# A fused linear-attention and feed-forward kernel: another order of the pair visits from stage 10 on

## The chip, the cores and the metric

The kernel runs on one core of one Trainium2 chip. The core has five engines with instruction streams of their own: TensorE (PE), which multiplies matrices into PSUM; VectorE (DVE) and ScalarE (ACT), which work element by element and can read PSUM; GpSimd (POOL), which here builds tiles in SBUF and issues loads; and SyncE (SP), which issues transposes and stores. They meet only at semaphores. The metric is the device time of one execution in microseconds; all times below are microseconds unless another unit stands beside them.

## The reference

For each batch and head a state of 48 x 48 is carried along 768 tokens (linear attention with a decay `w` and a bonus `u` for the present token). The result, 3072 x 384, goes through two dense products with a leaky ReLU between them.

```python
B, H, S, D = 4, 8, 768, 48
for t in range(S):
    cur = einsum('bhd,bhe->bhde', u * k[t], v[t])
    y[t] = einsum('bhd,bhde->bhe', r[t], state + cur)
    state = w[:, :, None] * state + einsum('bhd,bhe->bhde', k[t], v[t])
x = y.transpose(0, 2, 1, 3).reshape(3072, 384)
h = x @ w_in            # 384 -> 2048
out = maximum(0.01 * h, h) @ w_out   # 2048 -> 384
```

## The kernel before

**Stages.** The 768 tokens are cut into 6 chunks of 128, for 4 batches: 24 stages, numbered chunk by chunk, so stage n uses the state that stage n - 4 left. From about stage 8 on the stages are worked in pairs.

**Tokens of the order.** All work is recorded from one long string, `ORDER` (lines 27 to 52): each token calls a function that adds operations, and each engine executes its own operations in the order in which the string added them. The tokens that matter here, n being a stage (for J a pair):

- `k`, `r`, `v` n: loads, issued by POOL (L241).
- `Pnq`, `Pnk`: DVE scales r and k with decay tables (L390). `XnT`: SP transposes both by DMA into `tp` (L395).
- `qn`: three DVE operations, ku (L419), rku (L421) and a reduction to `s_tok` (L423), the weights of the present token. `Qn`: two POOL operations write them as diagonal tiles into `at` (L430).
- `An`: scores on PE, 8 matmuls into two PSUM banks (L482). `Mna`, `Mnb`: DVE copies the masked scores over the diagonal tiles in `at` (L495).
- `Kn`: key-value products on PE, 4 matmuls into one bank (L523). `Sn`: two DVE operations, one that adds the bank to the old state (L589) and one that applies the decay (L591). The result is the state of stage n + 4.
- `Yn`: the attention's output on PE, 28 matmuls in 32-column strips (L621) from v, `at`, `tp` and the state. `yn`: ACT copies it to `xT` (L635).
- `Jp.i`: an eighth of the first dense product of pair p on PE, 6 matmuls into one bank (L660); `jp.i`: ACT applies the leaky ReLU into `gT` (L671). It reads `xT` of both stages of the pair.
- `Hn`: the second dense product of stage n on PE, 16 matmuls into one bank (L684); `hn`: ACT copies it (L696) and SP stores it (L698). It needs all of `gT` of its stage.

**Waits.** `Sched` notes who wrote and who read each buffer and gives an operation waits on those of other engines that it needs. An engine executes in order, so an operation that waits holds up all behind it.

**PSUM banks.** The eight banks are a list. `take()` takes the first entry and `give()` appends one at its end. Both are called while the string is read: a bank given back by `Sn` is marked free from that place of the string on, and whoever takes it next waits for the operation that read it last. `Sn` calls `give` for the bank of `Kn`, `Mna` and `Mnb` for those of `An`, and `yn`, `jp.i` and `hn` for theirs.

Of the kernel before, what the change touches and what calls it, by code (L numbers as in the profile page):

```python
# [26 lines left out]
ORDER = """  # L27
w8 qk0 k0 v0z one r0 trow ones v0y tcol wlz r1 id8 F9 wi1 u8 zr table Cw Wl id E w bc lnw c0q@ T0q c0k@ tri u exps k1
T0k u16 wu8 Cu t0q t0k qtab P1q F6 k3 v3 U A0 ktab T1q v0 t1q X0 C D0 P1k T1k t1k F4 M0b P3k M0a T3k K3 utab X1 A1 D1
Q0 Y0 t3k P0k r3 P3q M1a T3q r2 P2q y0 k2 K0 M1b v1 Q1 W G0.1 Y1 t3q X3 wi3 A3 y1 g0.1 S3 T2q D3 G1.1 g1.1 k5 t2q r5 r4  # L30
P2k T2k wi2 S0 v2 M3b t2k Q3 G0.3 g0.3 G1.3 k4 M3a Y3 P5k A2 y3 P4q T4q v4 wi0 T5k v5 wo3 t4q g1.3 G3.1 q5 t5k Q5 G3.3
g3.3 P5q r6 wo2 X2 g3.1 M2b D2 wo1 G3.2 Q2 G0.2 g0.2 T5q t5q K2 P4k T4k M2a t4k S2 G1.2 g3.2 q4 Q4 K1 S1 Y2 A5 A4 G1.0
y2 G2.1 M5a G0.0 G2.3 M4a M5b Y5 g0.0 y5 M4b Y4 y4 G2.2 g2.2 K4 J2.4 j2.4 k6 wo0 J2.1 J2.2 g1.0 g1.2 S4 k7 P6q q6 j2.1
P6k P7k G2.0 r7 q7 X6T J2.6 j2.6 J2.3 j2.3 k8 G3.0 J2.7 j2.7 k9 r9 j2.2 J2.5 P7q g3.0 g2.3 X7T J2.0 H1 h1 r8 q8 g2.0 Q6
P9k j2.0 P8k H0 j2.5 H3 Q7 A6 P9q X9T P8q X8T v6 A7 M6a v7 M7a g2.1 H2 h2 v9 v11 v10 M6b Y6 M7b y6 Q8 q9 Y7 y7 K5 r11
K6 S6 r10 k10 S5 Q9 v8 K7 S7 h0 h3 k11 J3.0 j3.0 J3.1 j3.1 J3.2 j3.2 J3.3 j3.3 J3.4 j3.4 J3.5 j3.5 J3.6 j3.6 J3.7 j3.7
A8 A9 M8a M8b M9a M9b P10q P10k X10T P11q P11k X11T k12 r12 v12 k13 r13 v13 q10 Q10 q11 Q11 H4 h4 Y8 Y9 y8 y9 K8 K9 S8
S9 H5 h5 J4.0 j4.0 J4.1 j4.1 J4.2 j4.2 J4.3 j4.3 J4.4 j4.4 J4.5 j4.5 J4.6 j4.6 J4.7 j4.7 A10 A11 M10a M10b M11a M11b
P12q P12k X12T P13q P13k X13T k14 r14 v14 k15 r15 v15 q12 Q12 q13 Q13 H6 h6 Y10 Y11 y10 y11 K10 K11 S10 S11 H7 h7 J5.0
j5.0 J5.1 j5.1 J5.2 j5.2 J5.3 j5.3 J5.4 j5.4 J5.5 j5.5 J5.6 j5.6 J5.7 j5.7 A12 A13 M12a M12b M13a M13b P14q P14k X14T  # L40
P15q P15k X15T k16 r16 v16 k17 r17 v17 q14 Q14 q15 Q15 H8 h8 Y12 Y13 y12 y13 K12 K13 S12 S13 H9 h9 J6.0 j6.0 J6.1 j6.1
J6.2 j6.2 P16q P16k X16T P17q P17k X17T A14 A15 J6.3 j6.3 M14a M14b M15a M15b k18 r18 v18 k19 r19 v19 J6.4 j6.4 J6.5
j6.5 J6.6 j6.6 J6.7 j6.7 q16 Q16 q17 Q17 H10 h10 Y14 Y15 y14 y15 K14 K15 S14 S15 H11 h11 J7.0 j7.0 J7.1 j7.1 J7.2 j7.2
P18q P18k X18T P19q P19k X19T A16 A17 J7.3 j7.3 M16a M16b M17a M17b k20 r20 v20 k21 r21 v21 J7.4 j7.4 J7.5 j7.5 J7.6
j7.6 J7.7 j7.7 q18 Q18 q19 Q19 H12 h12 Y16 Y17 y16 y17 K16 K17 S16 S17 H13 h13 J8.0 j8.0 J8.1 j8.1 J8.2 j8.2 P20q P20k
X20T P21q P21k X21T A18 A19 J8.3 j8.3 M18a M18b M19a M19b k22 r22 v22 k23 r23 v23 J8.4 j8.4 J8.5 j8.5 J8.6 j8.6 J8.7
j8.7 q20 Q20 q21 Q21 H14 h14 Y18 Y19 y18 y19 K18 K19 S18 S19 H15 h15 J9.0 j9.0 J9.1 j9.1 J9.2 j9.2 P22q P22k X22T P23q
P23k X23T A20 A21 J9.3 j9.3 M20a M20b M21a M21b J9.4 j9.4 J9.5 j9.5 J9.6 j9.6 J9.7 j9.7 q22 Q22 q23 Q23 H16 h16 Y20 Y21
y20 y21 H17 h17 J10.0 j10.0 J10.1 j10.1 J10.2 j10.2 A22 A23 J10.3 j10.3 M22a M22b M23a M23b J10.4 j10.4 J10.5 j10.5
J10.6 j10.6 J10.7 j10.7 H18 h18 Y22 Y23 y22 y23 H19 h19 J11.0 j11.0 J11.1 j11.1 J11.2 j11.2 J11.3 j11.3 J11.4 j11.4  # L50
J11.5 j11.5 J11.6 j11.6 J11.7 j11.7 H20 h20 H21 h21 H22 h22
"""


# [750 lines left out]
```

## Time and profile before

| what | value |
|---|---|
| runs | 168.78, 168.86, 168.94 us; median 168.86 us |
| span of the profiled execution, first to last instruction | 166.8 us |
| instructions in it | 4840 |
| PE busy | 160.2 us |
| DVE, ACT, POOL busy | 107.6, 89.0, 111.0 us |
| granted TensorE clock, mean | 1.000 |

The profiled execution is one execution of the same program; its span leaves out what lies ahead of the first and behind the last instruction. In the rows of the timeline the first number is the start, counted from the span's beginning, the second the time from there to the end of the last of the merged instructions (`x16` means 16 of them), and a bracket at the end tells how long the engine was idle before the row and who released it. PEld is TensorE's loading of weights, which runs beside its matmuls. Ends of matmuls are modelled, so the prediction measures blocks of PE from start to start.

### The profile page before, as it was taken

What the parts mean: (1) busy time and instruction counts of PE and PEld (TensorE: products, weight loads), DVE (VectorE), ACT (ScalarE), POOL (GpSimd) and SP (SyncE); (2) the same over time, 40 slices, a digit from 0 to 9 for tenths busy, and PEclk for the clock granted to TensorE, in tenths of its full rate; (3) what the DMA queues carried; (4) which work ended last, traced back from release to release, by engine and by line L of the source; (5) the groups of instructions that cost most, each with busy time, mean ns of one, the idle gap of its engine ahead of it and who ended that gap; (6) DMA issues with size and microseconds to landing.
All of it is one profiled execution on the core that took longest, in us unless ns stands there. A gap on an engine that the chain in (4) does not pass through costs nothing.

```text
span 166.8 us, 4840 instructions
## 1 busy us (share of the span) xinstructions
PE 160.2 (96%) x2076; PEld 120.6 (72%) x2076; DVE 107.6 (64%) x224; ACT 89.0 (53%) x168; POOL 111.0 (67%) x125
## 2 busy tenths in 40 slices
PE   2899989999999999999999999999999999999994
PEld 2578879986567678678678678678678678678663
DVE  7799998478687695695699998865765705000000
ACT  3846973875048339339337437437437447449121
POOL 8999898978999949859759979896630630000000
PEclk9999999999999999999999999999999999999999
DMA  7999999999999994996994999999917011011012
GB/s 109 156 140 157 169 193 192 171 149 173 93 168 220 113 157 130 105 108 155 105 146 118 152 127 127 156 140 140 154 51 165 12 47 51 0 47 51 35 59 96
DMA packets 101267, 20.18 MB, mean 121 GB/s; under 512 B 94459, under 2 KB 101246, under 8 KB 101246
## 3 DMA queue, kind: packets, MB, share of 16 engines
q0 software_dynamic: 76512, 10.03, 95.0%
q1 hardware_dynamic: 23694, 9.65, 29.1%
q8 instruction: 16, 0.26, 0.7%
q10 hardware_dynamic: 1040, 0.20, 0.6%
q14 instruction: 5, 0.04, 0.1%
HBM read 20.45 MB, written 4.72 MB: 151 GB/s over the span
## 4 chain that ended last, share of the span: by engine, by line
PE 86%; POOL 7%; DMA 3%; DVE 2%; issue 0%; ACT 0%; POOLq 0%
PE ps L684 38%; PE ps L660 36%; PE ps L621 6%; DMA r_sb<-in_r_dram 3%; PE ps L482 3%; PE ps L523 2%; POOL r_sb L241 2%; POOL k_sb L241 2%; POOL v_sb L241 2%; POOL w_in_sb L251 1%; DVE prod L405 1%; DVE s_tok L423 0%; PE ps L453 0%; POOL trow L273 0%; DVE rku L421 0%
## 5 line engine op out<-in xcount | busy, mean ns | idle before, releaser
L660 PE MATMUL ps<-xT,w_in_sb 128*128 128x256 bf16 (+1 forms) x672 | 67.2, 257 | 0.0
L684 PE MATMUL ps<-w_out_sb,gT 128*128 128x384 bf16 (+2 forms) x400 | 65.6, 320 | 0.0
L671 ACT ACTIVATE gT<-ps 128x512 bf16<-128x512 f32 x96 | 56.3, 598 | 13.8 <-PE ps L660 9.7
L660 PEld LDWEIGHTS ps<-xT,w_in_sb 128*128 128x128 bf16 x672 | 57.1, 98 | 7.5 <-DVE sum_t L589 0.5
L430 POOL TENSOR_TENSOR at<-ident,s_tok 128x512 bf16<-128x512 bf16 x40 | 42.7, 1096 | 23.4 <-DVE s_tok L423 23.4
L684 PEld LDWEIGHTS ps<-w_out_sb,gT 128*128 128x128 bf16 x400 | 37.7, 98 | 22.4
L696 ACT ACTIVATE out_sb<-ps 128x384 f32<-128x384 f32 (+2 forms) x25 | 11.8, 477 | 54.5 <-PE ps L684 54.5
L495 DVE CAST_PREDICATED at<-mask,ps 128x512 bf16<-128x512 uint16 x40 | 24.9, 684 | 21.3 <-PE ps L482 21.2
L241 POOL DMA_DIRECT2D v_sb<-in_v_dram x24 | 22.1, 927 | 0.0
L241 POOL DMA_DIRECT2D k_sb<-in_k_dram x23 | 21.2, 925 | 0.0
L241 POOL DMA_DIRECT2D r_sb<-in_r_dram x23 | 21.1, 924 | 0.1
L421 DVE TENSOR_TENSOR rku<-r_sb,ku 128x384 bf16<-128x384 bf16 x20 | 13.8, 688 | 1.1 <-DMA r_sb<-in_r_dram 0.5
L589 DVE TENSOR_TENSOR sum_t<-ps,st 128x384 bf16<-128x384 f32 x16 | 8.8, 550 | 5.6 <-PE ps L523 5.6
L635 ACT ACTIVATE xT<-ps 128x384 bf16<-128x384 f32 x24 | 10.8, 490 | 2.6 <-PE ps L621 2.6
L423 DVE TENSOR_REDUCE s_tok<-rku 128x8 f32<-128x384 bf16 x20 | 11.1, 553 | 0.7
L591 DVE TENSOR_TENSOR st<-sum_t,wl 128x384 bf16<-128x384 bf16 x16 | 10.6, 664 | 0.6
L621 PE MATMUL ps<-at,v_sb 128*32 128x128 bf16 x384 | 10.8, 223 | 0.0
L390 DVE TENSOR_TENSOR qk<-k_sb,ktab 128x384 bf16<-128x384 bf16 x23 | 10.1, 444 | 1.1 <-DMA k_sb<-in_k_dram 1.1
L621 PEld LDWEIGHTS ps<-tp,st 128*32 128x32 bf16 x240 | 7.3, 96 | 3.0 <-issue 1.6
L621 PEld LDWEIGHTS ps<-at,v_sb 128*32 128x32 bf16 x384 | 8.8, 98 | 0.5 <-issue 0.2
L621 PE MATMUL ps<-tp,st 128*32 128x128 bf16 x240 | 9.1, 221 | 0.0
L390 DVE TENSOR_TENSOR qk<-r_sb,qtab 128x384 bf16<-128x384 bf16 x23 | 8.8, 386 | 0.2 <-DMA r_sb<-in_r_dram 0.2
(63 smaller groups left out, 92.9 us busy)
## 6 DMA issues: line engine op xcount, KB each, us to landing
out_dram<-out_sb SPq DMA_DIRECT2D x23, 192.0 KB, 2.2
v_sb<-in_v_dram POOLq DMA_DIRECT2D x24, 96.0 KB, 4.8
r_sb<-in_r_dram POOLq DMA_DIRECT2D x23, 96.0 KB, 4.7
k_sb<-in_k_dram POOLq DMA_DIRECT2D x23, 96.0 KB, 4.9
w_in_sb<-in_moe_w_in_dram POOLq DMA_DIRECT2D x4, 384.0 KB, 6.1
w_out_sb<-in_moe_w_out_dram POOLq DMA_DIRECT2D x4, 384.0 KB, 7.1
tp<-qk SPq DMA_TRANSPOSE x18, 5.3
k_f<-in_k_dram ACTq DMA_DIRECT2D x1, 192.0 KB, 2.8
```

Source lines behind the costliest of these rows:

```text
L241: add("pool", lambda: G.dma_start(dst, src), R=pace, W=[(which, n)], dma=f"{which}{n}")
L390: add("dve", lambda: V.tensor_tensor(qk[iq][:, H * half:H * half + H, 0:D], hd(src), hd(tab[:, :]), ALU.mult), R=[(name, n), "qk"[half] + ...
L421: add("dve", lambda: V.tensor_tensor(rku[i2][:, :], r_of(n), ku[i2][:, :], ALU.mult), R=[("r", n), ("ku", i2)], W=[("rku", i2)])
L423: add("dve", lambda: V.tensor_reduce(s_tok[i2][:, :], hd(rku[i2][:, :]), AX.X, ALU.add), R=[("rku", i2)], W=[("s", i2)])
L430: add("pool", lambda hh=hh, s_of=s_of: G.tensor_tensor(at[ia][:, hh, :, :], ident[:, :].unsqueeze(1).to_broadcast([128, NP, 128]), s_of.un ...
L495: add("dve", lambda: V.copy_predicated(at[n % NAT][:, hh, :, :], mask[:, :].bitcast(mybir.dt.uint16).unsqueeze(1).to_broadcast([128, NP, 1 ...
L621: last = PE.matmul(ps_y[32 * q:32 * q + 32, 128 * s:128 * s + 128], a, m, start=not whole and step == 0, stop=step == len(columns[q]) - 1)
L635: add("act", lambda: A.activation(xT[ix][:, :, 128 * slot:128 * slot + 128], ps_y[:, 0:HD].rearrange("p (s t) -> p s t", t=128), AF.Copy), ...
L660: last = PE.matmul(ps_g[:, step * f:step * f + step], w_in_sb[:, s, 128 * fb:128 * fb + 128], xT[ix][:, s, t], start=s == 0, stop=s == NSL ...
L671: add("act", lambda: A.activation(gT[ig][:, fb0:fb0 + count, t], ps_g[:, :].rearrange("p (f t) -> p f t", t=128 * width), AF.Prelu, alpha= ...
L684: last = PE.matmul(ps_o[:, 0:c1 - c0], gT[ig][:, s, 128 * slot:128 * slot + 128], w_out_sb[:, s, c0:c1], start=s == 0, stop=s == NFB - 1)
L696: add("act", lambda: A.activation(out_sb[io][:, c0:c1], ps_o[:, 0:c1 - c0], AF.Copy), R=[key], W=held)
```

## The change

Only the string is changed, from the end of J4 (the first dense product of stages 8 and 9) on. Before, the scores of a pair stand behind or inside the first products, in a visit of their own, and the other visit is H, both Y, both K, H:

```diff
 J4.0 j4.0 J4.1 j4.1 J4.2 j4.2 J4.3 j4.3 J4.4 j4.4 J4.5 j4.5 J4.6 j4.6 J4.7 j4.7
-A10 A11 M10a M10b M11a M11b P12q P12k X12T P13q P13k X13T k14 r14 v14 k15 r15 v15 q12 Q12 q13 Q13
-H6 h6 Y10 Y11 y10 y11 K10 K11 S10 S11 H7 h7
-J5.0 j5.0 J5.1 j5.1 J5.2 j5.2 J5.3 j5.3 J5.4 j5.4 J5.5 j5.5 J5.6 j5.6 J5.7 j5.7
-A12 A13 M12a M12b M13a M13b P14q P14k X14T P15q P15k X15T k16 r16 v16 k17 r17 v17 q14 Q14 q15 Q15
-H8 h8 Y12 Y13 y12 y13 K12 K13 S12 S13 H9 h9
-J6.0 j6.0 J6.1 j6.1 J6.2 j6.2 P16q P16k X16T P17q P17k X17T A14 A15 J6.3 j6.3 M14a M14b M15a M15b
...
+P12q P12k X12T P13q P13k X13T q12 q13
+A10 A11 M10a M10b M11a M11b k14 r14 v14 k15 r15 v15 Q12 Q13
+H6 h6 H7 h7 K10 K11 Y10 Y11 y10 y11 A12 A13 M12a M12b M13a M13b
+P14q P14k X14T P15q P15k X15T q14 q15
+J5.0 j5.0 J5.1 j5.1 k16 r16 v16 k17 r17 v17 Q14 Q15 S10 S11
+J5.2 j5.2 J5.3 j5.3 J5.4 j5.4 J5.5 j5.5 J5.6 j5.6 J5.7 j5.7
+H8 h8 H9 h9 K12 K13 Y12 Y13 y12 y13 A14 A15 M14a M14b M15a M15b
+P16q P16k X16T P17q P17k X17T q16 q17
+J6.0 j6.0 J6.1 j6.1 k18 r18 v18 k19 r19 v19 Q16 Q17 S12 S13
+J6.2 j6.2 J6.3 j6.3 J6.4 j6.4 J6.5 j6.5 J6.6 j6.6 J6.7 j6.7
...
+H16 h16 H17 h17 Y20 Y21 y20 y21 A22 A23 M22a M22b M23a M23b
+J10.0 j10.0 J10.1 j10.1 J10.2 j10.2 J10.3 j10.3 J10.4 j10.4 J10.5 j10.5 J10.6 j10.6 J10.7 j10.7
 H18 h18 Y22 Y23 y22 y23 H19 h19 J11.0 j11.0 J11.1 j11.1
```

The lines are set here visit by visit; the string has them in other line breaks. In the new order the visit of a pair is both H of the pair two before, both K, both Y, the scores of the next pair, and then all eight J of this pair. The key-value products of stages 20 to 23 are not needed, so the last visits have no K, and the end from H18 on is as before. The same tokens are called, each once; the order of POOL's and SP's operations is the same in both kernels, that of PE, DVE and ACT differs.

More of the change, by code (lines that the diff above doesn't have):

```diff
@@ L29 @@
 T0k u16 wu8 Cu t0q t0k qtab P1q F6 k3 v3 U A0 ktab T1q v0 t1q X0 C D0 P1k T1k t1k F4 M0b P3k M0a T3k K3 utab X1 A1 D1
[L30 to L48, printed above, removed]
@@ L49 @@
-y20 y21 H17 h17 J10.0 j10.0 J10.1 j10.1 J10.2 j10.2 A22 A23 J10.3 j10.3 M22a M22b M23a M23b J10.4 j10.4 J10.5 j10.5
-J10.6 j10.6 J10.7 j10.7 H18 h18 Y22 Y23 y22 y23 H19 h19 J11.0 j11.0 J11.1 j11.1 J11.2 j11.2 J11.3 j11.3 J11.4 j11.4
-J11.5 j11.5 J11.6 j11.6 J11.7 j11.7 H20 h20 H21 h21 H22 h22
+Q0 Y0 t3k P0k r3 P3q M1a T3q r2 P2q y0 k2 K0 M1b v1 Q1 W G0.1 Y1 t3q X3 wi3 A3 y1 g0.1 S3 T2q D3 G1.1 g1.1 k5 t2q r5
+r4 P2k T2k wi2 S0 v2 M3b t2k Q3 G0.3 g0.3 G1.3 k4 M3a Y3 P5k A2 y3 P4q T4q v4 wi0 T5k v5 wo3 t4q g1.3 G3.1 q5 t5k Q5
@@ new lines @@
+G3.3 g3.3 P5q r6 wo2 X2 g3.1 M2b D2 wo1 G3.2 Q2 G0.2 g0.2 T5q t5q K2 P4k T4k M2a t4k S2 G1.2 g3.2 q4 Q4 K1 S1 Y2 A5 A4
+G1.0 y2 G2.1 M5a G0.0 G2.3 M4a M5b Y5 g0.0 y5 M4b Y4 y4 G2.2 g2.2 K4 J2.4 j2.4 k6 wo0 J2.1 J2.2 g1.0 g1.2 S4 k7 P6q q6
+j2.1 P6k P7k G2.0 r7 q7 X6T J2.6 j2.6 J2.3 j2.3 k8 G3.0 J2.7 j2.7 k9 r9 j2.2 J2.5 P7q g3.0 g2.3 X7T J2.0 H1 h1 r8 q8
+g2.0 Q6 P9k j2.0 P8k H0 j2.5 H3 Q7 A6 P9q X9T P8q X8T v6 A7 M6a v7 M7a g2.1 H2 h2 v9 v11 v10 M6b Y6 M7b y6 Q8 q9 Y7 y7
+K5 r11 K6 S6 r10 k10 S5 Q9 v8 K7 S7 h0 h3 k11 J3.0 j3.0 J3.1 j3.1 J3.2 j3.2 J3.3 j3.3 J3.4 j3.4 J3.5 j3.5 J3.6 j3.6
@@ new lines @@
+J3.7 j3.7 A8 A9 M8a M8b M9a M9b P10q P10k X10T P11q P11k X11T k12 r12 v12 k13 r13 v13 q10 Q10 q11 Q11 H4 h4 Y8 Y9 y8
+y9 K8 K9 S8 S9 H5 h5 J4.0 j4.0 J4.1 j4.1 J4.2 j4.2 J4.3 j4.3 J4.4 j4.4 J4.5 j4.5 J4.6 j4.6 J4.7 j4.7 P12q P12k X12T
+P13q P13k X13T q12 q13 A10 A11 M10a M10b M11a M11b k14 r14 v14 k15 r15 v15 Q12 Q13 H6 h6 H7 h7 K10 K11 Y10 Y11 y10 y11
+A12 A13 M12a M12b M13a M13b P14q P14k X14T P15q P15k X15T q14 q15 J5.0 j5.0 J5.1 j5.1 k16 r16 v16 k17 r17 v17 Q14 Q15
+S10 S11 J5.2 j5.2 J5.3 j5.3 J5.4 j5.4 J5.5 j5.5 J5.6 j5.6 J5.7 j5.7 H8 h8 H9 h9 K12 K13 Y12 Y13 y12 y13 A14 A15 M14a
@@ new lines @@
+M14b M15a M15b P16q P16k X16T P17q P17k X17T q16 q17 J6.0 j6.0 J6.1 j6.1 k18 r18 v18 k19 r19 v19 Q16 Q17 S12 S13 J6.2
+j6.2 J6.3 j6.3 J6.4 j6.4 J6.5 j6.5 J6.6 j6.6 J6.7 j6.7 H10 h10 H11 h11 K14 K15 Y14 Y15 y14 y15 A16 A17 M16a M16b M17a
+M17b P18q P18k X18T P19q P19k X19T q18 q19 J7.0 j7.0 J7.1 j7.1 k20 r20 v20 k21 r21 v21 Q18 Q19 S14 S15 J7.2 j7.2 J7.3
+j7.3 J7.4 j7.4 J7.5 j7.5 J7.6 j7.6 J7.7 j7.7 H12 h12 H13 h13 K16 K17 Y16 Y17 y16 y17 A18 A19 M18a M18b M19a M19b P20q
+P20k X20T P21q P21k X21T q20 q21 J8.0 j8.0 J8.1 j8.1 k22 r22 v22 k23 r23 v23 Q20 Q21 S16 S17 J8.2 j8.2 J8.3 j8.3 J8.4
@@ new lines @@
+j8.4 J8.5 j8.5 J8.6 j8.6 J8.7 j8.7 H14 h14 H15 h15 K18 K19 Y18 Y19 y18 y19 A20 A21 M20a M20b M21a M21b P22q P22k X22T
+P23q P23k X23T q22 q23 J9.0 j9.0 J9.1 j9.1 Q22 Q23 S18 S19 J9.2 j9.2 J9.3 j9.3 J9.4 j9.4 J9.5 j9.5 J9.6 j9.6 J9.7 j9.7
+H16 h16 H17 h17 Y20 Y21 y20 y21 A22 A23 M22a M22b M23a M23b J10.0 j10.0 J10.1 j10.1 J10.2 j10.2 J10.3 j10.3 J10.4
+j10.4 J10.5 j10.5 J10.6 j10.6 J10.7 j10.7 H18 h18 Y22 Y23 y22 y23 H19 h19 J11.0 j11.0 J11.1 j11.1 J11.2 j11.2 J11.3
+j11.3 J11.4 j11.4 J11.5 j11.5 J11.6 j11.6 J11.7 j11.7 H20 h20 H21 h21 H22 h22
```

## The prediction

> **What bounds the kernel now.** I read the page first: busy shares, the clock row, the chain of waits.
>
> ```profile
> PE 160.2 (96%) x2076; PEld 120.6 (72%) x2076; DVE 107.6 (64%) x224; ACT 89.0 (53%) x168; POOL 111.0 (67%) x125
> PEclk9999999999999999999999999999999999999999
> PE 86%; POOL 7%; DMA 3%; DVE 2%; issue 0%; ACT 0%; POOLq 0%
> ```
>
> TensorE is busy 96% of the span at the full granted clock, and the chain that ended last is 86% PE. In order of time, the last piece of that chain that is not PE, apart from some hundredths and the last copy, is
>
> ```profile
> 20.35 1.20 DVE prod L405
> ```
>
> so the rest lies ahead of 22 us, which the change does not touch. So in the stages concerned only two things count: the sum of PE's own work, and any wait that appears on PE where there was none. VectorE (DVE) has slack on average, but that says nothing on the place of its work.
>
> Next the timeline of one pair's period, from the scores A10 A11 to A12 A13 and on to the next outputs. PE rows give the start of each block (the first of its matmuls):
>
> ```profile
> 67.57 0.62 PE L482 MATMUL ps<-tp 48*128 48x128 bf16 x16
> ...
> 70.83 0.24 PE L621 MATMUL ps<-tp,st 128*32 128x128 bf16 x4
> ...
> 71.72 0.51 PE L523 MATMUL ps<-v_sb,qk 128*128 128x96 bf16 x8
> 72.07 2.76 PE L684 MATMUL ps<-w_out_sb,gT 128*128 128x384 bf16 x16
> 74.67 5.40 PE L660 MATMUL ps<-xT,w_in_sb 128*128 128x256 bf16 x48
> 80.01 0.62 PE L482 MATMUL ps<-tp 48*128 48x128 bf16 x16
> 80.56 2.77 PE L684 MATMUL ps<-w_out_sb,gT 128*128 128x384 bf16 x16
> 83.27 0.24 PE L621 MATMUL ps<-tp,st 128*32 128x128 bf16 x4
> ```
>
> From start to start: A pair 0.55 (80.01 to 80.56), H 2.71 ahead of Y (80.56 to 83.27) but 2.60 ahead of J (72.07 to 74.67), Y pair 0.89 (70.83 to 71.72), K pair 0.35, J 5.34. They add to the period, 80.01 - 67.57 = 12.44, with no wait in it. The difference 2.71 - 2.60 = 0.11 is what PE pays when the next block uses another tiling of its array (A: two row halves; Y: four column strips; J, H, K: the whole array). Its weight loads stand idle there:
>
> ```profile
> 80.00 0.45 PEld L482 LDWEIGHTS ps<-tp 48*128 48x128 bf16 x16 [0.21 <-issue]
> 83.26 0.10 PEld L621 LDWEIGHTS ps<-tp,st 128*32 128x32 bf16 x4 [0.32 <-issue]
> ```
>
> Then DVE and GpSimd (POOL) behind A12 A13 at 80.01:
>
> ```profile
> 74.77 0.55 DVE L589 TENSOR_TENSOR sum_t<-ps,st 128x384 bf16<-128x384 f32 x1
> ...
> 80.52 2.48 DVE L495 CAST_PREDICATED at<-mask,ps 128x512 bf16<-128x512 uint16 x4 [3.01 <-PE ps L482]
> 82.92 0.35 DVE L390 TENSOR_TENSOR qk<-r_sb,qtab 128x384 bf16<-128x384 bf16 x1
> ...
> 83.99 0.35 DVE L419 TENSOR_TENSOR ku<-k_sb,u_tab 128x384 bf16<-128x384 bf16 x1
> 84.38 0.36 DVE L421 TENSOR_TENSOR rku<-r_sb,ku 128x384 bf16<-128x384 bf16 x1
> 84.77 0.55 DVE L423 TENSOR_REDUCE s_tok<-rku 128x8 f32<-128x384 bf16 x1
> ...
> 85.41 4.32 POOL L430 TENSOR_TENSOR at<-ident,s_tok 128x512 bf16<-128x512 bf16 x4 [2.85 <-DVE s_tok L423]
> 85.62 1.08 DVE L421 TENSOR_TENSOR rku<-r_sb,ku 128x384 bf16<-128x384 bf16 x1
> 86.74 0.55 DVE L423 TENSOR_REDUCE s_tok<-rku 128x8 f32<-128x384 bf16 x1
> 87.21 0.55 DVE L589 TENSOR_TENSOR sum_t<-ps,st 128x384 bf16<-128x384 f32 x1
> 88.75 0.54 DVE L589 TENSOR_TENSOR sum_t<-ps,st 128x384 bf16<-128x384 f32 x1
> ```
>
> The reader is to see DVE's order: four masks, four P products, six q operations, then the pair's first L589 (S). From the first score matmul to the end of that L589 are 87.21 + 0.55 - 80.01 = 7.75; one period earlier 74.77 + 0.55 - 67.57 = 7.75 as well.
>
> **The change, part by part.** Removed or added: no instruction at all; it is an order. On POOL and SP the sequences stay as they are; PE, DVE and ACT change.
>
> PE. Old period: A, H, Y, K, H, J, with four changes of tiling (into A, out of it, into Y, out of it). New: H, H, K, Y, A, J, with three (into Y, Y to A, out of A). One less saves 0.11 in each of six visits (pairs 10/11 to 20/21): 0.66 if PE alone decides. In new blocks: H 2.60 each, K 0.35 + 0.11 = 0.46, Y 0.89, A 0.55, J 5.34 - 0.11 = 5.23 since H follows.
>
> xT. J now comes 0.55 after Y, where K and an H lay between. What is queued ahead of it is only A; what J needs is both ACT copies of Y. A place where ACT was idle ahead of them shows how late they are:
>
> ```profile
> 28.44 0.24 PE L621 MATMUL ps<-tp,st 128*32 128x128 bf16 x4
> ...
> 29.07 0.88 ACT L635 ACTIVATE xT<-ps 128x384 bf16<-128x384 f32 x2 [0.59 <-PE ps L621]
> ```
>
> They end at 29.95, 1.51 after Y's first matmul; with 0.06 to wake PE (row below) J can start at 1.57, where PE is ready at 0.89 + 0.55 = 1.44. So 0.13 per visit, which about eats the saved 0.11. From below this wait is 0, if the copies overlap A entirely. The copy of the second H stands ahead of them on ACT:
>
> ```profile
> 74.93 0.49 ACT L696 ACTIVATE out_sb<-ps 128x384 f32<-128x384 f32 x1 [2.60 <-PE ps L684]
> ```
>
> It ends 75.42 - 74.67 = 0.75 after the start of the block behind that H; the first Y's share ends later (0.46 for K and half of Y's 0.89), so it adds nothing.
>
> K's banks, where I see the decisive step. A K pair holds two of the eight PSUM banks until S reads them (L589). Banks are handed out in the order in which they were given back. Followed through the new list: A12 A13 take four, J5.0 and J5.1 the two that Y10 Y11 left, J5.2 to J5.5 those of the masks, J5.6 and J5.7 again Y's, and H8 the bank of K10, H9 that of K11. So H8 must wait for S10's L589, and H9 for S11's; the same for H10, H12, H14, H16 with S12 to S18. In the old list J5.5 took K10's bank: at about 74.67 + 5 x 0.65 = 77.9, against a read that ended at 75.32, with 2.6 to spare. And in the new list S10 stands on DVE behind M12 M13, P14 P15 and q14 q15: the very sequence of the rows above, begun by A12 A13. Hence, counted from A's first matmul: L589 ends at 7.75. That PE waits on exactly this read, and how fast it wakes, stands already in one place:
>
> ```profile
> 52.45 0.55 DVE L589 TENSOR_TENSOR sum_t<-ps,st 128x384 bf16<-128x384 f32 x1
> ...
> 53.05 0.55 PEld L660 LDWEIGHTS ps<-xT,w_in_sb 128*128 128x128 bf16 x6 [0.31 <-DVE sum_t L589]
> ```
>
> The read ended at 53.00, the load came at 53.05 and its matmul about 0.01 later (as at 80.00 and 80.01): 0.06. H8 starts at 7.75 + 0.06 = 7.81. PE would have been ready at 0.55 + 0.13 + 5.23 = 5.91. The wait is 1.90. Behind it on PE's queue stand H9, K12, K13, Y12, Y13, A14 A15 and J6, and with A14 the next masks, so the next chain on DVE starts that much later: nothing is caught up. H9 needs S11's L589, by 88.75 + 0.54 - 80.01 = 9.28, and is ready at 7.81 + 2.60 = 10.41: no further wait. Then 5.20 for two H, 0.46, 0.89 to the next A: a period of 7.81 + 5.20 + 0.46 + 0.89 = 14.36 against 12.44, so 1.92 more. The xT wait and the saving ahead of J lie inside it. It holds from A12, A14, A16, A18 and A20 (without K both sides lose 0.35): 5 x 1.92 = 9.60.
>
> The uncertain term is the second rku. Its line, with minimum, median and maximum in ns:
>
> ```profile
> L421 DVE TENSOR_TENSOR rku<-r_sb,ku x20: 357/359/2332, 19.1 to 131.0; 128x384 bf16<-128x384 bf16 x20
> ```
>
> This one takes 1.08 because POOL builds the pair's first diagonal tile at that time (85.41), which it starts as soon as the first s_tok is there. The bounds are 0.36 and one row where POOL came later and two tile operations fell on it:
>
> ```profile
> 94.95 2.33 DVE L421 TENSOR_TENSOR rku<-r_sb,ku 128x384 bf16<-128x384 bf16 x1
> ```
>
> I take 1.08, since in the new order POOL waits for s_tok as it does at 85.41: its six loads fit in front. In the first period they do so with little to spare:
>
> ```profile
> 64.79 0.94 POOL L241 DMA_DIRECT2D k_sb<-in_k_dram  x1
> ...
> 69.19 0.93 POOL L241 DMA_DIRECT2D v_sb<-in_v_dram  x1
> ```
>
> They end at 70.12; Q12 Q13 then take 4.32 and the next six loads 70.12 - 64.79 = 5.33, to 79.8, against an s_tok at about A12 (74.67) + 85.41 - 80.01 = 80.07. The Trainium skill (GPSIMD Engine Reference, Specifications) says that POOL shares its SBUF interfaces with VectorE and contends with DVE instructions that have two SBUF inputs. This rule speaks against the change, as it lengthens a chain that PE now waits for; by it the sum keeps the 1.08, without it each period would lose 0.72. The rows agree: 0.36 at 84.38 without a tile operation, 1.08 at 85.62 beside one.
>
> The rest is covered. P12 P13 and q12 q13 now run ahead of M10 M11; there DVE idled 3.02:
>
> ```profile
> 68.08 1.29 DVE L495 CAST_PREDICATED at<-mask,ps 128x512 bf16<-128x512 uint16 x2 [3.02 <-PE ps L482]
> ```
>
> With four P at 0.27 apart and six q in about 2.5 (1.25 from one ku to the next) they need 3.6, so M10 starts about 0.6 late; Y10 needs it only after two H (5.2), of which the masks take 2.5. Without that cover the 0.6 would count once. The transposes, the loads and the diagonal tiles all come earlier against their users than before. The wait of J5.2 for M12's first mask (done at 1.2 after A) comes at 0.68 + 1.31 = 1.99 and is none.
>
> Ends: the first visit (A12 follows Y11) saves 0.11, the last J10 waits 0.13. Sum: 9.60 - 0.11 + 0.13 = 9.62. The profiled span is 166.8 and the runs 168.78 to 168.94, so some 2.0 lie around the span; I leave them as they are. 166.8 + 9.6 + 2.0 = 178.5.
>
> **The rivals.** *No wait at the bank, and it ends not slower*: it needs L589 by 5.85 after A instead of 7.75; for that DVE's six q operations would have to be gone. Then per visit -0.11 + 0.13: 168.9, or with no xT wait either, 168.86 - 0.66 = 168.2. For it: PE does all the work; against it: two rows of 7.75. The Trainium skill (TensorEngine Tiling, Key Properties) says that changing the tiling mode drains TensorE, and the 0.11 agrees; by that rule alone the answer is 168.2. Chance 0.04 for 168.9 and 0.03 for 168.2.
>
> *POOL is out of the way*: rku at 0.36, so the wait is 1.18 and the total 178.5 - 5 x 0.72 = 174.9. For it: the small margin of the loads; against: POOL idled 2.85 there. Chance 0.09.
>
> *POOL is late*, two tile operations on the rku in most periods: 1.25 more each, 178.5 + 6.2 = 184.7 in all five. For it the row at 94.95, against it that it is one in 20. Chance 0.05; in one or two periods, 179.7 to 181.0, it is part of the forecast.
>
> *The clock falls behind each wait*: PE idles 1.9 of 14.36 five times. If each H8 ran at half clock, 2.60 more each: 191.5. Against it:
>
> ```profile
> 0.00:4.00 4.00, 1.14 (x9) 0.88 (x9) 2.95 (x14) 1.28 (x1) 3.31 (x10) 1.00 0.67 108
> ```
>
> PE busy 1.14 of 4.00 and the granted clock (third last) 1.00. The Trainium skill (TensorE: Matmul & The Clock Gate, A second HAM failure mode) describes a kernel whose short idles at PSUM banks let the clock oscillate. No row here shows that. Chance 0.02.
>
> **How the numbers follow.** The forecast, 178.5, has 0.77. Range 174.9 to 181.0: below, the rku at 0.36 in all periods; above, two periods at 2.33. What is left out is the case of no wait (0.07), POOL late throughout (0.05) and the clock (0.02). About 0.2%, 0.3 us, is what a measurement of this kernel tells from none. Faster by more: 0.03; within: 0.04; slower: 0.93.
>
> **What would show it.** In the new profile the waits should name PE at L684 released by DVE sum_t L589, five times, near 1.9 each and 9.5 in total; PE's busy time should stay near 160 while its share falls to about 91%; the scores should follow each other by 14.4. J right behind A should start 1.57 after Y's first matmul. PE unbroken through H8, or a wait there that names ACT or a transpose, would make the prediction wrong in its mechanism; L589 ending at another distance than 7.75 from A, with the same wait, in its size only.

## The result, and the profile after

| | before | after |
|---|---|---|
| median of the runs, us | 168.9 (6 runs, 168.69 to 170.41) | 178.31 (6 runs, 178.18 to 178.54) |
| span of the profiled execution, us | 166.8 | 176.4 |
| ratio after to before | | 1.0523, 95% interval 1.0477 to 1.0569 |

The kernel became slower by 9.4 us by the medians, 5.6%; 178.5 was forecast. (The ratio of the table is an estimate over the runs of both kernels and not the ratio of the two medians, which is 1.0557; its interval holds both.) The page of the profile after shows where, at a glance:

```profile
PE 160.4 (91%) x2076; PEld 120.9 (69%) x2076; DVE 107.6 (61%) x224; ACT 89.3 (51%) x168; POOL 111.2 (63%) x125
...
PEclk9999999999999999999999999999999999999999
...
PE 70%; DVE 23%; issue 2%; DMA 2%; ACT 1%; SPq 1%; DVEq 0%
```

Each engine does the work it did before (PE 160.4 us against 160.2) at the same clock, in a longer span. In the chain that ended last PE falls from 86% to 70%, and VectorE, 2% before, now has 23%: it has come onto the path. The list of waits names the place (engine, line, whom it waited for, total, number, longest):

```profile
PEld ps L684 <- DVE sum_t L589: 10.0, 5, 2.0
PE ps L684 <- DVE sum_t L589: 8.6, 5, 1.7
...
PEld ps L660 <- ACT xT L635: 1.5, 7, 0.2
```

Five waits of the second product H on the VectorE operation that reads a key-value bank. (PE and PEld count the same five idle times; for PE the modelled ends of the matmuls before are taken off. From start to start a wait is 1.89, as worked out further below.) The timeline of one period after, PE's rows:

```profile
68.17 5.37 PE L684 MATMUL ps<-w_out_sb,gT 128*128 128x384 bf16 x32
73.38 0.50 PE L523 MATMUL ps<-v_sb,qk 128*128 128x96 bf16 x8
...
73.81 0.24 PE L621 MATMUL ps<-tp,st 128*32 128x128 bf16 x4
...
74.71 0.62 PE L482 MATMUL ps<-tp 48*128 48x128 bf16 x16
75.38 5.41 PE L660 MATMUL ps<-xT,w_in_sb 128*128 128x256 bf16 x48
82.52 5.37 PE L684 MATMUL ps<-w_out_sb,gT 128*128 128x384 bf16 x32 [1.72 <-DVE sum_t L589]
87.72 0.50 PE L523 MATMUL ps<-v_sb,qk 128*128 128x96 bf16 x8
89.06 0.62 PE L482 MATMUL ps<-tp 48*128 48x128 bf16 x16
```

and VectorE's and POOL's of the same stretch:

```profile
75.22 2.48 DVE L495 CAST_PREDICATED at<-mask,ps 128x512 bf16<-128x512 uint16 x4 [3.42 <-PE ps L482]
77.62 0.35 DVE L390 TENSOR_TENSOR qk<-r_sb,qtab 128x384 bf16<-128x384 bf16 x1
...
80.11 4.32 POOL L430 TENSOR_TENSOR at<-ident,s_tok 128x512 bf16<-128x512 bf16 x4 [0.65 <-DVE s_tok L423]
...
80.33 1.08 DVE L421 TENSOR_TENSOR rku<-r_sb,ku 128x384 bf16<-128x384 bf16 x1
81.44 0.55 DVE L423 TENSOR_REDUCE s_tok<-rku 128x8 f32<-128x384 bf16 x1
81.91 0.55 DVE L589 TENSOR_TENSOR sum_t<-ps,st 128x384 bf16<-128x384 f32 x1
```

The reader is to see the loop that closes here: scores A12 A13 at 74.71, masks, P, q, and then S10's L589, which ends at 82.46, and 0.06 later H8 starts. From the scores to H8 it is 82.52 - 74.71 = 7.81, and from these scores to the next 89.06 - 74.71 = 14.35.

The start-up varies from run to run: the scores of stage 8, from which on the kernels compared here begin to differ soon, come at 55.1 in some profiled executions and above 56 in others. So beside each kernel's time I give the stretch of its chain of waits from those scores to the last copy of the output. Before:

```profile
55.20 0.55 PE ps L482 x16
...
164.52 0.28 ACT out_sb L696
```

which is 164.52 - 55.20 = 109.32 us, and after:

```profile
55.25 0.55 PE ps L482 x16
...
174.10 0.28 ACT out_sb L696
```

118.85 us, 9.53 more. A table at the end of the next section has this stretch for all kernels. Each experiment's time stands beside that of the kernel before, measured along with it, and the bracket behind a ratio is its 95% interval.

### The profile page after: what moved, and what is told of

Read it like the earlier page. It is cut to its first block, busy times and chain, and to the rows that moved or that the text cites. A ratio compares the mean times of both kernels' runs of the same rounds, so it can differ in the third digit from the quotient of the medians.

```text
span 176.4 us, 4845 instructions
## 1 busy us (share of the span) xinstructions
PE 160.4 (91%) x2076; PEld 120.9 (69%) x2076; DVE 107.6 (61%) x224; ACT 89.3 (51%) x168; POOL 111.2 (63%) x125
## 4 chain that ended last, share of the span: by engine, by line
PE 70%; DVE 23%; issue 2%; DMA 2%; ACT 1%; SPq 1%; DVEq 0%
PE ps L684 36%; PE ps L660 19%; DVE at L495 6%; PE ps L621 5%; DVE rku L421 4%; DVE qk L390 4%; DVE s_tok L423 3%; PE ps L482 3%; PE ps L523 2%; DMA w_row<-in_w_dram 2%; DVE ku L419 2%; PE ps L453 2%; DVE sum_t L589 1%; DVE prod L405 1%; DVE at L491 1%
## 5 line engine op out<-in xcount | busy, mean ns | idle before, releaser
L684 PE MATMUL ps<-w_out_sb,gT 128*128 128x384 bf16 (+2 forms) x400 | 64.7, 320 | 8.6 <-DVE sum_t L589 8.6
L660 PE MATMUL ps<-xT,w_in_sb 128*128 128x256 bf16 (+1 forms) x672 | 66.5, 257 | 0.4
L684 PEld LDWEIGHTS ps<-w_out_sb,gT 128*128 128x128 bf16 x400 | 37.7, 98 | 32.9 <-DVE sum_t L589 10.0
L421 DVE TENSOR_TENSOR rku<-r_sb,ku 128x384 bf16<-128x384 bf16 x20 | 12.2, 611 | 1.7 <-DMA r_sb<-in_r_dram 1.0
L591 DVE TENSOR_TENSOR st<-sum_t,wl 128x384 bf16<-128x384 bf16 x16 | 12.7, 794 | 0.5
L635 ACT ACTIVATE xT<-ps 128x384 bf16<-128x384 f32 x24 | 10.8, 491 | 4.0 <-PE ps L621 3.9
L423 DVE TENSOR_REDUCE s_tok<-rku 128x8 f32<-128x384 bf16 x20 | 11.1, 553 | 0.7
L589 DVE TENSOR_TENSOR sum_t<-ps,st 128x384 bf16<-128x384 f32 x16 | 8.8, 548 | 2.4 <-PE ps L523 2.4
L419 DVE TENSOR_TENSOR ku<-k_sb,u_tab 128x384 bf16<-128x384 bf16 x20 | 7.9, 394 | 1.3 <-DMA k_sb<-in_k_dram 1.3
```

The costliest lines, as they stand in the source:

```text
L421: add("dve", lambda: V.tensor_tensor(rku[i2][:, :], r_of(n), ku[i2][:, :], ALU.mult), R=[("r", n), ("ku", i2)], W=[("rku", i2)])
L423: add("dve", lambda: V.tensor_reduce(s_tok[i2][:, :], hd(rku[i2][:, :]), AX.X, ALU.add), R=[("rku", i2)], W=[("s", i2)])
L591: add("dve", lambda: V.tensor_tensor(new[:, :, :], sum_t[n % 4][:, :, :], wl[:, :, :], ALU.mult), R=[("sum", n % 4), "wl0", "wl1"], W=[("s ...
L660: last = PE.matmul(ps_g[:, step * f:step * f + step], w_in_sb[:, s, 128 * fb:128 * fb + 128], xT[ix][:, s, t], start=s == 0, stop=s == NSL ...
L684: last = PE.matmul(ps_o[:, 0:c1 - c0], gT[ig][:, s, 128 * slot:128 * slot + 128], w_out_sb[:, s, c0:c1], start=s == 0, stop=s == NFB - 1)
```

## The experiments

**The bank alone.** A kernel whose five engines execute exactly the sequences of the changed one; only the place of the string at which S gives K's banks back is later. Since there is nothing for VectorE between the two places, its order stays. The same edit is made for S12 to S19.

```diff
-... J5.1 j5.1 k16 r16 v16 k17 r17 v17 Q14 Q15 S10 S11 J5.2 j5.2 ... J5.7 j5.7 H8 h8 H9 h9 K12 K13
+... J5.1 j5.1 k16 r16 v16 k17 r17 v17 Q14 Q15 J5.2 j5.2 ... J5.7 j5.7 S10 S11 H8 h8 H9 h9 K12 K13
```

> All five instruction streams are those of the changed kernel; only the place in the string where S10 to S19 give their banks back is later, so H8 takes the bank of J5.2 instead of K10's. If the bank wait is the whole cause (theory), the wait of PE at L684 for L589 is gone, the period falls from 14.35 to about 12.46 and the time by about 9.5, to 168.8 us. If the order of the blocks itself costs the time (tiling changes, J right behind A, the clock), the time stays near 178.3. If POOL beside VectorE is the cause, VectorE's sequence is as late as before and the time stays near 178.3 too.

Measured: 169.26 us against 168.97, ratio 1.0021 (0.9999 to 1.0043). No wait of L684 is left in the list of waits. PE's rows of the timeline:

```profile
75.89 0.62 PE L482 MATMUL ps<-tp 48*128 48x128 bf16 x16
76.55 5.41 PE L660 MATMUL ps<-xT,w_in_sb 128*128 128x256 bf16 x48
81.80 5.36 PE L684 MATMUL ps<-w_out_sb,gT 128*128 128x384 bf16 x32
87.00 0.50 PE L523 MATMUL ps<-v_sb,qk 128*128 128x96 bf16 x8
88.33 0.62 PE L482 MATMUL ps<-tp 48*128 48x128 bf16 x16
```

H8 follows J at 76.55 + 5.25 = 81.80 without a break, and the period is 88.33 - 75.89 = 12.44, as before the change. So the whole loss hangs on which bank H takes; the order of the blocks on PE as such adds 0.04 to the chain, and to the time at most the 0.43% that the interval allows.

**VectorE's order alone.** The banks go to the same takers as in the changed kernel (H8 has K10's), but S stands ahead of q on VectorE.

```diff
-... X15T q14 q15 J5.0 j5.0 J5.1 j5.1 k16 r16 v16 k17 r17 v17 Q14 Q15 S10 S11 J5.2
+... X15T J5.0 j5.0 J5.1 j5.1 k16 r16 v16 k17 r17 v17 S10 S11 q14 q15 Q14 Q15 J5.2
```

> The banks go to the same takers as in the changed kernel (H8 still takes K10's bank and waits for S10), but on VectorE S10 S11 stand ahead of q14 q15 instead of behind them, in all five periods. Theory: L589 ends about 0.51 + 2.40 + 1.07 + 0.55 = 4.5 after A's first matmul, ahead of H8's readiness at 5.9, so the wait vanishes and the time is about 168.8 us. If the bank's reuse alone costs something whatever VectorE's order, the time stays near 178.3.

Measured: 169.43 us against 168.97, ratio 1.0022 (0.9993 to 1.0052). Its timeline:

```profile
74.95 0.62 PE L482 MATMUL ps<-tp 48*128 48x128 bf16 x16
...
78.93 0.55 DVE L589 TENSOR_TENSOR sum_t<-ps,st 128x384 bf16<-128x384 f32 x1
...
80.86 2.44 PE L684 MATMUL ps<-w_out_sb,gT 128*128 128x384 bf16 x14
```

The read ends 79.48 - 74.95 = 4.53 after the scores and H8 comes at 5.91, when PE is ready for it (its row has 14 matmuls because the view ends there). So the cost needs both: that H takes K's bank, and that this bank's reader stands at the end of VectorE's chain. Either edit alone removes it.

**One wait instead of five.** The late return of the banks for S12 to S19 alone, so that of the H only H8 and H9 still take banks of K, and H9 has no wait.

> The changed kernel with the banks of S12 to S19 given back later, so that only H8 still waits, for S10. Theory: one wait of five is left, nothing behind it catches up: 168.9 + 1.9 = 170.8 us, with one wait of PE at L684 on L589. If a single wait is absorbed by slack elsewhere, 168.9; if the first wait alone brings on the rest, near 178.

Measured: 171.19 us against 169.09, ratio 1.0121 (1.0092 to 1.0149), with one wait:

```profile
PE ps L684 <- DVE sum_t L589: 1.7, 1, 1.7
```

Its stretch of the chain is 1.94 longer than that of the kernel before. Against the kernel with all banks returned late, one wait costs 111.26 - 109.36 = 1.90 and five cost 118.85 - 109.36 = 9.49: nothing behind a wait is caught up, and they add.

**POOL out of the way of the second rku.** POOL builds the pair's tiles in the other order, so it needs the later s_tok first.

```diff
-... k16 r16 v16 k17 r17 v17 Q14 Q15 ...
+... k16 r16 v16 k17 r17 v17 Q15 Q14 ...
```

> From stage 14 on POOL builds the diagonal tiles of the pair in the other order (Q15 before Q14), so it starts only when both reductions are done, and VectorE's second rku runs alone. Theory: this rku takes 0.36 instead of 1.08, L589 ends 7.03 instead of 7.75 after A, each wait is 0.72 shorter and the time is 178.3 - 5 x 0.72 = 174.7 us. If POOL beside VectorE is no part of the chain, the time stays at 178.3.

Measured: 174.99 us against 168.97, ratio 1.0344 (1.0316 to 1.0373). Its timeline:

```profile
80.21 0.36 DVE L421 TENSOR_TENSOR rku<-r_sb,ku 128x384 bf16<-128x384 bf16 x1
80.60 0.55 DVE L423 TENSOR_REDUCE s_tok<-rku 128x8 f32<-128x384 bf16 x1
81.07 0.55 DVE L589 TENSOR_TENSOR sum_t<-ps,st 128x384 bf16<-128x384 f32 x1
81.24 2.15 POOL L430 TENSOR_TENSOR at<-ident,s_tok 128x512 bf16<-128x512 bf16 x2 [1.90 <-DVE s_tok L423]
```

The rku takes 0.36, POOL starts behind both reductions, and the stretch of the chain is 3.61 shorter than after the change: 5 x 0.72. So 0.72 of each wait was VectorE being held up by POOL.

**The second H between A and J.** An attempt at a faster kernel: no bank wait (S right behind K), one tiling change fewer than before, and an H that hides the xT copies.

```diff
-H6 h6 H7 h7 K10 K11 Y10 Y11 y10 y11 A12 A13 M12a M12b M13a M13b ... q14 q15 J5.0 j5.0 ... S10 S11 J5.2
+H6 h6 K10 K11 S10 S11 Y10 Y11 y10 y11 A12 A13 M12a M12b M13a M13b ... q14 q15 H7 h7 J5.0 j5.0 ... J5.2
```

> Two edits from the changed kernel: S10 to S19 stand right behind K (VectorE reads K's banks before the masks), and the second H of each of six visits stands between A and J. Theory: no bank wait; three tiling changes per visit instead of four in the kernel before save 6 x 0.11 = 0.66 us and the xT copies are hidden by that H, so the time is about 168.2 us, faster than the kernel before (168.9). If a tiling change costs nothing beyond what the kernel before pays, or new waits eat it, the time is 168.9 or above.

Measured: 171.23 us against 168.97, ratio 1.012 (1.0087 to 1.0152), and not the 168.2 that was expected. Its chain of waits has one long piece that is not PE, in the first visit:

```profile
67.37 7.30 DMA tp<-qk
...
74.81 0.40 PE ps L482 x8
```

A13 waited for its transposed tile. The transposes of stages 12 and 13 are issued from 66.08 on, and with an H moved behind A the scores came earlier: A12 starts at 72.77, 4.75 behind A10, where it starts 7.09 behind it after the change (74.71 - 67.62). PE idled 1.64 ahead of A13. A smaller part is another wait: Y11 was held up 0.24 by the last mask of M11, since one H does not cover the late masks as two did. The later visits run as meant; the chain's pieces from one scores block to the next are

```profile
86.99 0.55 PE ps L482 x16
...
99.33 0.55 PE ps L482 x16
...
111.66 0.55 PE ps L482 x16
```

12.34 and 12.33, against 12.44 before the change.

**The same from the second visit on.** The first visit keeps the changed kernel's order, with the banks of S10 S11 returned late.

> As the kernel with the second H between A and J, except in the first visit (A12 A13), which keeps the changed kernel's order with the banks of S10 S11 given back later, so that A13 comes 2.6 us later. Theory: what cost 2 us there was only the second transpose of that first visit, which landed 1.64 us too late for A13; without it five visits save 0.11 each by one tiling change fewer, and the first is even (0.11 saved, 0.13 waited for xT): 168.9 - 0.55 = 168.3 to 168.4 us. If that order loses in every visit, the time stays above 169.5.

Measured: 169.02 us against 169.09, ratio 0.9989 (0.9965 to 1.0013). The profiled execution's chain is 0.47 shorter than before, close to the 0.53 of the terms, but the runs' spread (167.94 to 169.53) covers it. Run again:

> The kernel with the second H between A and J from the second visit on, once more, to narrow its interval. By the chain of its profile it is 0.47 us shorter than the kernel before from the scores of stage 8 to the end, 0.28%: ratio 0.997. If the gain is not there, the ratio is 1.000.

Measured: 168.78 us against 169.19, ratio 0.9972 (0.9937 to 1.0007). In its profiled execution the stretch is only 0.10 shorter, since A15 came late once:

```profile
86.63 0.25 PEld L482 LDWEIGHTS ps<-tp 48*128 48x128 bf16 x8 [0.39 <-ACT xT L635]
```

The profile names ACT, whose copy ends at the same moment, but A15 needs a transposed tile and not xT, and its two banks were read for the last time by 85.46. The second transpose of that visit was issued at 81.0 and landed 5.5 later, at 86.5; A15's first load follows about 0.1 behind it, as A13's, at 74.78, followed the landing at 74.67 in the kernel with H between A and J. So the transpose is the releaser here too. Both medians lie below those of the kernel before, both intervals contain 1: a gain of some tenths of a microsecond is likely and not shown.

**What holds up a rku when POOL only loads.** In the first visit after the change, and in all seven runs of kernels above, the rku of stage 13 took 1.08, though POOL's rows have no tile operation there. (In the kernel before, this rku, at 73.18, stood beside a tile operation.) After the change:

```profile
67.51 0.91 POOL L241 DMA_DIRECT2D k_sb<-in_k_dram  x1
67.74 1.08 DVE L421 TENSOR_TENSOR rku<-r_sb,ku 128x384 bf16<-128x384 bf16 x1
68.39 0.91 POOL L241 DMA_DIRECT2D r_sb<-in_r_dram  x1
```

The experiment swaps Q12 and Q13 too:

> As the kernel with the tiles built in the other order, and now also Q13 before Q12. In every trace so far the rku of stage 13 took 1.08 although POOL's rows show only loads beside it (no tile operation before 70). If what stretches it is Q12, ready but still behind the loads in POOL's queue, this rku falls to 0.36, since Q13 is not ready yet; if it is a load, it stays at 1.08. No change of the time is expected from it (M10 is covered by two H): about 175 us.

Measured: 175.92 us in one run, with a late start (stage 8's scores at 56.54); its stretch of the chain, 115.24, is that of the kernel without this last swap. The rku:

```profile
68.80 0.92 POOL L241 DMA_DIRECT2D k_sb<-in_k_dram  x1
69.03 0.36 DVE L421 TENSOR_TENSOR rku<-r_sb,ku 128x384 bf16<-128x384 bf16 x1
```

It falls to 0.36 with the same load beside it. That is one trace, against eight in which Q12 comes first and the rku takes 1.08.

All kernels, by the stretch from stage 8's scores to the last copy (us; the difference is to the kernel before):

| kernel | stage 8's scores | last copy | stretch | difference | by the terms of the prediction |
|---|---|---|---|---|---|
| before | 55.20 | 164.52 | 109.32 | | |
| after | 55.25 | 174.10 | 118.85 | 9.53 | 9.62 |
| banks returned late | 56.42 | 165.78 | 109.36 | 0.04 | 6 x (0.13 - 0.11) = 0.12 |
| S ahead of q | 55.48 | 164.84 | 109.36 | 0.04 | 0.12 |
| one wait left | 56.34 | 167.60 | 111.26 | 1.94 | 1.92 + 0.10 = 2.02 |
| tiles swapped | 55.13 | 170.37 | 115.24 | 5.92 | 9.62 - 3.60 = 6.02 |
| H between A and J | 55.65 | 166.40 | 110.75 | 1.43 | -0.66 |
| the same from the second visit | 55.29 | 164.14 | 108.85 | -0.47 | -0.53 |
| the same, run again | 56.70 | 165.92 | 109.22 | -0.10 | -0.53 |
| tiles swapped from stage 12 on | 56.54 | 171.78 | 115.24 | 5.92 | 6.02 |

## Why the prediction was right

The forecast was 178.5 and the median is 178.31. By its steps:

*The bank wait.* Forecast: five waits, H8 at 7.81 after A, 1.90 each, a period of 14.36. Measured: five, 7.81, and 14.35. PE was ready at 75.38 + 5.25 (J, as in the kernel with the banks returned late) = 80.63, so the wait was 1.89. The first two experiments show that it is the cause, and the one with a single wait that the five add.

*The chain of 7.75.* Taken from the old trace, where the same operations stood in the same order on VectorE behind the same scores, but with S12 at the end in place of S10. It is what made the size exact: 82.46 - 74.71 = 7.75.

*The second rku.* Forecast 1.08 with bounds 0.36 and 2.33. In the kernel after, minimum, median and maximum of the line are

```profile
L421 DVE TENSOR_TENSOR rku<-r_sb,ku x20: 357/359/1083, 19.2 to 137.7; 128x384 bf16<-128x384 bf16 x20
```

so the late case (2.33) did not occur, and POOL idled 0.65 ahead of its tiles in the first period (80.11), where the forecast saw some 0.3. That first period was a close call, and that it fell on the right side is in part luck: in the kernel with H between A and J POOL's loads of that visit ended only at 80.03, and the second rku, at 80.00, took 2.33. In the later periods POOL idled 4.76 or more. That the term is real the swapped tiles show: 3.61 for five.

*xT.* Forecast: J 1.57 after Y's first matmul. Measured: 75.38 - 73.81 = 1.57; the list of waits has it as PEld's waits on ACT at L635, 0.2 at most. As forecast it does not count in the periods with a bank wait.

*The tiling change.* 0.11 each, one less per visit. The periods with H between A and J show it, 12.33 against 12.44. K to Y took 73.81 - 73.38 = 0.43, with 0.46 forecast, and Y to A 74.71 - 73.81 = 0.90, with 0.89. The sum was 0.09 too high, of which five periods of 14.35 for 14.36 are about half. Most of the rest of the 0.19 lies in the 2.0 taken for what is around the span: the profiled execution after has 178.24 against a span of 176.4, which is 1.8.

*The cover of q12 and q13.* Here a number was off without consequence: M10 was to start 0.6 late and started 69.32 - 68.13 = 1.2 late (0.51 after the scores at 67.62 would be 68.13), because the rku of stage 13 took 1.08 and not 0.36. Two H behind covered that as well. One H would not have: in the kernel with H between A and J, Y11 waited 0.24 for it.

*The rivals.* No wait at the bank: that came about only in other kernels, where H takes another bank or the bank is read earlier, and there the chain is 0.04 longer than before, so the wait for xT and the saved tiling change cancel. POOL out of the way: that is the kernel with the tiles swapped, 174.99 where this rival had 174.9. POOL late throughout: no rku of the kernel after took more than 1.08. The clock: the granted clock stayed at 1.000 with five idle times of 1.9 us in the span. The drain rule of the Trainium skill (TensorEngine Tiling (Array Packing), Key Properties) agrees with the 0.11 and was no guide to the result, since a wait lay on top of it.

## What to carry to other kernels

Where buffers come from a first-in first-out list, moving work also moves who inherits which buffer: for each step that a reorder brings forward, ask whose buffer it takes, who reads that buffer last, and what stands ahead of this reader on its engine. If the old trace has the same sequence behind the same trigger, its distance (here 7.75 us) can be set against the time at which the waiting engine would be ready (5.91), and the difference, with the 0.06 that PE takes to wake, is the price per round. The cheapest cure can be one that moves no instruction at all: returning the buffer later, so that somebody takes it who needs it later.

## What the runs showed of the hardware that was not expected

A VectorE operation with two SBUF inputs was held up (1.08 us in place of 0.36), as the swap of Q12 and Q13 indicates, by a POOL tile operation that, by POOL's rows, had not begun: its input was ready, but it stood behind loads in POOL's queue, from 67.51 to 70.15 in the kernel after. With a tile first whose input was not yet ready, the same rku beside the same kind of load took 0.36. The Trainium skill (GPSIMD Engine Reference, Specifications) says that POOL shares SBUF interfaces with VectorE and contends with instructions of two SBUF inputs; the numbers agree with that, and this pair of traces suggests that the time of the hold goes by when the tile operation becomes ready rather than by its row. Whether POOL's rows are displaced or the interface is taken ahead of the work these runs do not tell.

The rku was not the only operation stretched. The decay step of S (L591), also with both inputs in SBUF, took 1.03 and 0.61 at 82.49 and 84.03 beside POOL's tile operations, and 0.36 at 79.51 in the kernel with S ahead of q, where POOL had none. The reduction L423, with one input, and L589, with one input in PSUM, kept their 0.55 in every row of the kernels before and after (0.54 to 0.56).
